# Loading the second head of every V tile through ScalarE's DMA queue in a decode attention kernel

## The chip, the core and the metric

The kernel runs on one core of a Trainium2 chip. A core has five engines that run side by side: TensorE (PE, matrix multiplication into PSUM), VectorE (DVE), ScalarE (ACT), GpSimd (POOL) and SyncE (SP). Data comes from device memory by DMA transfers, which SyncE or ScalarE issue, each into a queue of its own, and which 16 DMA engines carry out. The metric is the time of one execution in microseconds (us); lower is better.

## What is computed

One decode step of an attention block and of an MLP, both on the same normalised row, for a batch of four:

```
xn = layernorm(x)                          # x: 4 x 1 x 576
# attention: 32 query heads, 16 K/V heads, head size 128, the last 2048 positions of the cache
q = (xn @ wq) as 32 heads
p = softmax(q . k / sqrt(128))             # k: 4 x 16 x 2048 x 128, every K/V head serves 2 query heads
A = (p . v) @ wo                           # v as k
# MLP; with one position the shifted parts are zero, so x1 = xn
B = xn + gelu(layernorm(xn) @ w3) @ w4     # w3: 576 x 4608, w4: 4608 x 576
out = x + A + B
```

K and V of the window are 33.5 MB each in bf16; with the weights the kernel reads some 87 MB.

## The kernel before

All large loads go through a ring of four buffers of 4 MB, the pool `big`. In order they hold wq, K tile 0, half of w3, K tile 1, the rest of w3 with a part of w4, K tiles 2 to 7, V tiles 0 to 7, and the rest of w4 (`w4_end`). A load into a buffer can be issued only when the tile that was there four places earlier has been read: V tile 0 waits for the transposes of K tile 4, V tile 4 for the last matmul on V tile 0, and `w4_end` for V tile 4. A second, small pool holds the tiles of wo.

The work has three stages:

1. **K stage** (L518 to L535). For each of the eight K tiles of 4 MB, VectorE transposes it in four instructions (L298), and TensorE multiplies it with the queries (L305) into four banks of scores. Between them stand the products with w3, the gelu and a first part of w4.
2. **Softmax** (L154 to L201). ScalarE takes exponentials (L322), VectorE and ScalarE scale them (L343, L341), TensorE transposes them (L347), and VectorE and ScalarE copy them to the tile `PZ` (L355, L352).
3. **V stage** (L551 to L578). A V tile holds two heads, 2 MB each, loaded by one DMA each (L119 in `v_load`). The heads 0 to 15 go in order, and TensorE's order is written by hand (`manual_schedule`). For each head, `v_compute` runs 16 matmuls (L385), then `head_out` sums four diagonal blocks on VectorE (L422, L424), and one head later TensorE transposes the sum (L434). After four heads, `select` sorts the rows (L445 on TensorE, L453 and L454 on VectorE), and `project` multiplies with a tile of wo (L396). Selection and projection of heads 8 to 11 are placed behind head 12's matmuls and ahead of head 13's. Ahead of head 14's stand eight matmuls that fold partial sums (L561); the sums are copied by ScalarE (L555, L556).

At the end come the transposed sum and selection of heads 12 to 15, then the matmuls of `w4_end` and the last tile of wo (L414), the cast (L591) and the store (L592).

Apart from the small load of x (L98), every DMA is issued by SyncE, in program order: K tiles (L110), V (L119), wo (L405) and w4 (L573, L495). The V tiles 0 to 3 stand ahead of the softmax in the program, and tile 4 and later ones are issued behind heads 1, 3, 5 and 7. Completion is counted on eight semaphores that the loads use in turn, so a load also waits for the eighth before it to have landed.

Of the kernel before, what the change touches and what calls it, by code (L numbers as in the profile page):

```python
# [20 lines left out]
def kernel(  # L21
# [19 lines left out]
    nc = tc.nc  # L41
# [9 lines left out]
    G = 32  # L51
# [19 lines left out]
    v_win = A_v_cache[:, :, Sk - W:Sk, :]  # L71
# [43 lines left out]
    def v_load(pair):  # L115
        t = big.tile([P, 2, NCH, Dh], BF16, tag="big", name=f"v{pair}")
        for i in range(2):
            h = 2 * pair + i
            nc.sync.dma_start(out=t[:, i, :, :].rearrange("p c d -> p (c d)"),  # L119
                              in_=v_win[:, h].rearrange("b (p c) d -> p b (c d)", p=G))  # L120
            V_tiles[h] = t[:, i, :, :]

    wq_src = A_wq[0:KJ * P, :].rearrange("(p j) n -> p j n", j=KJ)
# [415 lines left out]
    for pair in range(NV0):  # L539
        v_load(pair)  # L540
        if pair % 2:
            load_wo(pair // 2)
    PZ = softmax()

    with tc.manual_schedule(engines={mybir.EngineType.PE}):
# [5 lines left out]
        for v in range(Hkv):  # L551
            run_projects()
            if v == Hkv - 3:
                sums = ktp.tile([P, DH], F32, tag="kt", name="sums")
                nc.scalar.copy(out=sums[0:64, :], in_=ACC[0:64, 0:DH])  # L555
                nc.scalar.copy(out=sums[64:P, :], in_=ACC2[64:P, 0:DH])  # L556
            if v == Hkv - 2:
                for q in range(2):
                    for z in range(2):
                        g = 2 * q + z  # L560
                        nc.tensor.matmul(out=ACC3[32 * g:32 * g + G, 0:DQ], lhsT=perm[:, q, :],  # L561
                                         rhs=sums[:, z * DQ:(z + 1) * DQ], start=False, stop=False, skip_group_check=True)
            v_compute(v)
            if selects:
                tsum, select = selects.pop()
                tsum()
                select()
            head_out(v)

            if v == 9:  # L570
                w4_end = big.tile([P, 2 * NFH - NE0, D], BF16, tag="big", name="w4_end")
                n0 = NFH - NE0
                nc.sync.dma_start(out=w4_end[:, 0:2 * n0, :].rearrange("p (e i) n -> p e (i n)", e=2), in_=w4_both)  # L573
                end = [(w4_end[:, e * n0:(e + 1) * n0, :], e, (1 - e) * NE0, n0) for e in range(2)]
            if v in (5, 9):
                load_wo((v + 3) // 4)
            if v % 2 and v // 2 + NV0 < Hkv // 2:
                v_load(v // 2 + NV0)  # L578
# [44 lines left out]
```

## Time and profile before

| | |
|---|---|
| Time, median of the runs shown | 213.42 us (213.35 to 213.48) |
| Time of the profiled execution | 213.12 us |
| Its span in the profile | 211.3 us |
| TensorE busy | 97.6 us (46%) |
| VectorE busy | 129.1 us (61%) |
| ScalarE busy | 17.8 us (8%) |
| Bytes read, mean rate | 87.17 MB, 413 GB/s |
| V loads at L119 | 16, 2048 KB each, 24.5 us from issue to landing (median) |

The span is what the profiler saw of the execution; 1.8 us lie around it. Busy shares are averages over stages with different limits, so they don't say which engine sets the time. For that one reads the slices (busy share of each engine in 40 equal parts of the span), the chain of waits (from the last instruction back to what released it) and the timeline of one engine, where the idle time before an instruction stands in brackets with what ended it. All times in these views are microseconds from the span's start.

### The profile page before, as it was taken

What the parts mean: (1) busy time and instruction counts of PE and PEld (TensorE: products, weight loads), DVE (VectorE), ACT (ScalarE), POOL (GpSimd) and SP (SyncE); (2) the same over time, 40 slices, a digit from 0 to 9 for tenths busy, and PEclk for the clock granted to TensorE, in tenths of its full rate; (3) what the DMA queues carried; (4) which work ended last, traced back from release to release, by engine and by line L of the source; (5) the groups of instructions that cost most, each with busy time, mean ns of one, the idle gap of its engine ahead of it and who ended that gap; (6) DMA issues with size and microseconds to landing.
All of it is one profiled execution on the core that took longest, in us unless ns stands there. A gap on an engine that the chain in (4) does not pass through costs nothing.

```text
span 211.3 us, 2591 instructions
## 1 busy us (share of the span) xinstructions
PE 97.6 (46%) x1099; PEld 49.8 (24%) x1099; DVE 129.1 (61%) x226; ACT 17.8 (8%) x36; POOL 1.8 (1%) x8
## 2 busy tenths in 40 slices
PE   1433159429703333423333330677499543553563
PEld 0110137408201011101111100543234221221252
DVE  7902692095359898879696951997836452135240
ACT  0003200000000000000000008951000000010000
POOL 2100000000000000000000000000000000000000
PEclk9999999999965555555555555589956785557555
DMA  7999999999999999999999999999999999999991
GB/s 299 397 471 422 406 450 394 449 410 470 409 447 434 406 453 428 416 459 416 416 425 403 440 426 433 412 437 431 418 419 431 426 419 428 437 406 428 422 386 49
DMA packets 5638, 87.32 MB, mean 413 GB/s; under 512 B 632, under 2 KB 636, under 8 KB 1532
## 3 DMA queue, kind: packets, MB, share of 16 engines
q1 hardware_dynamic: 5620, 87.17, 97.1%
q8 instruction: 8, 0.13, 0.3%
q14 instruction: 2, 0.02, 0.0%
q10 hardware_dynamic: 8, 0.00, 0.0%
HBM read 87.17 MB, written 0.00 MB: 413 GB/s over the span
## 4 chain that ended last, share of the span: by engine, by line
DMA 56%; DVE 27%; PE 8%; issue 4%; ACT 3%; SPq 1%; DVEq 0%; ACTq 0%
DMA k<-in_A_k_cache_dram 32%; DVE kt L298 19%; DMA w_end<-in_B_w_dram 12%; DMA v<-in_A_v_cache_dram 12%; PE S L305 4%; DVE prs L343 4%; PE O L385 2%; ACT E L322 2%; DVE osum L424 1%; DVE PZ L355 1%; DVE osum L422 1%; PE OT L434 1%; PE ACC L396 1%; PE pt L347 1%; SPq L136 1%
## 5 line engine op out<-in xcount | busy, mean ns | idle before, releaser
L298 DVE STREAM_TRANSPOSE kt<-k 128x2048 int32<-128x2048 int32 x32 | 71.1, 2279 | 15.9 <-DMA k<-in_A_k_cache_dram 15.9
L305 PE MATMUL S<-kt,qz 128*32 128x512 bf16 x256 | 30.4, 622 | 58.9 <-DVE kt L298 58.9
L385 PE MATMUL O<-v,PZ 128*32 128x512 bf16 x256 | 25.0, 513 | 12.9 <-DMA v<-in_A_v_cache_dram 12.1
L305 PEld LDWEIGHTS <-qz 128*32 128x32 bf16 x256 | 9.4, 127 | 75.8 <-issue 69.4
L422 DVE TENSOR_SCALAR osum<-O,diag 128x128 f32<-128x128 f32 x16 | 5.6, 349 | 22.7 <-PE O L385 22.7
L424 DVE SCALAR_TENSOR_TENSOR osum<-O,diag,osum 128x128 f32<-128x128 f32 x48 | 16.4, 345 | 0.8
L385 PEld LDWEIGHTS <-PZ 128*32 128x32 bf16 x256 | 7.2, 117 | 21.6 <-DMA v<-in_A_v_cache_dram 11.6
L322 ACT ACTIVATE E<-S,nb 128x256 f32<-128x256 f32 x8 | 4.5, 704 | 72.4 <-DVE nb L319 72.4
L347 PE MATMUL pt<-ident,prs 128*128 128x128 bf16 x64 | 5.9, 269 | 9.3 <-DVE prs L343 9.3
L434 PEld LDWEIGHTS OT<-sel,osum 128*128 128x128 f32 x32 | 6.2, 243 | 13.2 <-DVE osum L424 8.1
L434 PE MATMUL OT<-sel,osum 128*128 128x8 f32 x32 | 7.7, 314 | 3.2 <-DVE osum L424 3.2
L343 DVE TENSOR_SCALAR prs<-E,rdm 128x512 bf16<-128x512 f32 x12 | 8.0, 823 | 0.0
L347 PEld LDWEIGHTS <-prs 128*128 128x128 bf16 x64 | 5.2, 123 | 10.9 <-ACT prs L341 9.4
L317 DVE TENSOR_REDUCE mx<-S 128x1 f32<-128x512 f32 x4 | 2.8, 691 | 8.0 <-PE S L305 8.0
L478 PEld LDWEIGHTS <-w3a 128*128 128x128 bf16 x108 | 6.9, 166 | 1.7 <-issue 1.7
L478 PE MATMUL ACC<-ln2T,w3a 128*128 128x4 bf16 x108 | 7.0, 202 | 0.0
L396 PE MATMUL ACC<-wo,onx 128*4 128x288 bf16 x48 | 3.4, 433 | 7.4 <-DVE onx L454 7.4
L253 DVE CAST q_rows<-qp 128x256 bf16<-128x256 f32 x4 | 1.5, 418 | 8.5 <-PE qp L238 6.5
L436 DVE CAST on<-OT 128x8 bf16<-128x8 f32 x16 | 2.7, 166 | 5.6 <-PE OT L434 5.6
L238 PE MATMUL qp<-wq,xnT 128*8 128x512 bf16 x32 | 3.6, 628 | 3.6 <-DMA wq<-in_A_wq_dram 3.6
L341 ACT ACTIVATE prs<-E,rdm 128x512 bf16<-128x512 f32 x4 | 4.9, 1413 | 0.8 <-DVE rdm L329 0.8
L478 PEld LDWEIGHTS <-w3b 128*128 128x128 bf16 x72 | 4.5, 166 | 0.8 <-issue 0.8
(90 smaller groups left out, 67.3 us busy)
## 6 DMA issues: line engine op xcount, KB each, us to landing
k<-in_A_k_cache_dram SPq DMA_DIRECT2D x8, 4096.0 KB, 29.9
v<-in_A_v_cache_dram SPq DMA_DIRECT2D x16, 2048.0 KB, 24.5
wo<-in_A_wo_dram SPq DMA_DIRECT2D x4, 1152.0 KB, 29.8
wq<-in_A_wq_dram SPq DMA_DIRECT2D x1, 4096.0 KB, 12.7
w3a<-in_B_w_dram SPq DMA_DIRECT2D x1, 2304.0 KB, 26.8
w3b<-in_B_w_dram SPq DMA_DIRECT2D x1, 2304.0 KB
w_end<-in_B_w_dram SPq DMA_DIRECT2D x1, 2016.0 KB, 31.8
w3b<-in_B_w_dram SPq DMA_DIRECT2D x1, 1584.0 KB
```

What stands on the lines that cost most here:

```text
L298: nc.vector.transpose(out=ap32(kt[e], c0 * 2 * G, [[2 * G, C2 // 2], [1, 2], [2, G]]), in_=ap32(kn, c0 * 4 * G + e * G, [[4 * G, C2 // 2], ...
L305: nc.tensor.matmul(out=S[kq][c:c + 32, :].rearrange("p (c q l) -> p c q l", q=4, l=2), lhsT=qz[:, bp, m, y, :], rhs=kt[e][:, :, 4 * m:4 * ...
L322: nc.scalar.activation(out=E[:, :, g, x:GK:2].rearrange("p (c l) q -> p c q l", l=2), in_=S[g][:, 256 * x:256 * (x + 1)].rearrange("p (c q ...
L341: nc.scalar.mul(out=dst, in_=src, mul=rdm[:, b:b + 1])
L343: nc.vector.tensor_scalar_mul(out=dst, in0=src, scalar1=rdm[:, b:b + 1])
L347: nc.tensor.transpose(out=tp[:, cc, :], in_=pr[:, half * HC + cc, :, :, :].rearrange("p g k b -> p (g k b)"), identity=ident[:])
L385: nc.tensor.matmul(out=bank[G * j:G * j + G, :], lhsT=PZ[:, hp, c0:c0 + NI, :].rearrange("p c m -> p (c m)"), rhs=vn[:, c0:c0 + NI, :].rea ...
L396: nc.tensor.matmul(out=ACCS[half][o0:o0 + B, 0:DH], lhsT=lhsT, rhs=rhs_cols(q * DH, (q + 1) * DH), start=False, stop=False, skip_group_che ...
L422: nc.vector.tensor_scalar_mul(out=osum[:], in0=bank[:, 0:Dh], scalar1=diag[:, 0:1])
L424: nc.vector.scalar_tensor_tensor(out=osum[:], in0=bank[:, i * Dh:(i + 1) * Dh], scalar=diag[:, i:i + 1], in1=osum[:], op0=ALU.mult, op1=AL ...
L434: nc.tensor.matmul(out=OT[:, NB * o:NB * o + NB], lhsT=osum[:], rhs=sel[:], start=True, stop=True, skip_group_check=True)
L478: nc.tensor.matmul(out=gp[:, fc, :], lhsT=lhsT, rhs=rhs, start=False, stop=False, skip_group_check=True)
```

## The change

In `v_load`, the load of the second head of each V tile is issued by ScalarE instead of SyncE. The buffers, the bytes and the computation stay as they are.

```diff
         t = big.tile([P, 2, NCH, Dh], BF16, tag="big", name=f"v{pair}")
         for i in range(2):
             h = 2 * pair + i
-            nc.sync.dma_start(out=t[:, i, :, :].rearrange("p c d -> p (c d)"),
-                              in_=v_win[:, h].rearrange("b (p c) d -> p b (c d)", p=G))
+            queue = nc.scalar if i else nc.sync
+            queue.dma_start(out=t[:, i, :, :].rearrange("p c d -> p (c d)"),
+                            in_=v_win[:, h].rearrange("b (p c) d -> p b (c d)", p=G))
             V_tiles[h] = t[:, i, :, :]
```

In the built program ScalarE's eight new loads stand as follows: those of V tiles 0, 1 and 2 ahead of the exponentials (L322), that of tile 3 between the exponentials and the scaling (L341), and those of tiles 4 to 7 behind the last copy to `PZ` (L352) and ahead of the copies of L555 and L556. On SyncE the other loads keep their order. The semaphores still go round in program order over both queues. On VectorE all twelve scalings (L343) now stand ahead of the copies to `PZ` (L355), where before seven, three, one and one of them stood between these.

## The prediction

> **What bounds the kernel now.** I read the page's slices first, then the queues, the chain of waits, and TensorE's timeline at the end.
>
> ```profile
> DMA  7999999999999999999999999999999999999991
> ...
> q1 hardware_dynamic: 5620, 87.17, 97.1%
> ...
> q10 hardware_dynamic: 8, 0.00, 0.0%
> ```
>
> The 16 DMA engines are busy in every slice but the first and last, and one queue, SyncE's q1, carries all the data. ScalarE's queue q10 carried eight small packets, the load of x. So the time is 87 MB at some 428 GB/s, plus what follows the last landing. The chain of waits (start, us, what) says where it ends:
>
> ```profile
> 156.53 25.03 DMA v<-in_A_v_cache_dram
> 181.57 0.02 issue
> 181.58 26.28 DMA w_end<-in_B_w_dram
> 207.86 0.04 issue
> 207.91 0.46 PE ACC L414 x6
> 208.36 0.02 issue
> 208.38 0.31 DVE fin L591
> ```
>
> The last piece of w4 lands at 207.86, and only six small matmuls, the cast and the store follow. For every earlier transfer the computation finishes inside the time of the transfers behind it. Whether that stays true is the question, so the timeline of TensorE at the end counts (start, length, line, operation; in brackets the idle time before and what ended it):
>
> ```profile
> 181.61 1.90 PE L385 MATMUL O<-v,PZ 128*32 128x512 bf16 x16 [5.27 <-DMA v<-in_A_v_cache_dram]
> ...
> 187.15 1.13 PE L396 MATMUL ACC<-wo,onx 128*4 128x288 bf16 x16 [2.48 <-DVE onx L454]
> 188.07 1.92 PE L385 MATMUL O<-v,PZ 128*32 128x512 bf16 x16
> 189.92 0.39 PE L434 MATMUL OT<-sel,osum 128*128 128x8 f32 x2
> 190.24 0.45 PE L561 MATMUL ACC<-sums,perm 128*32 128x144 f32 x8
> 191.41 1.05 PE L385 MATMUL O<-v,PZ 128*32 128x512 bf16 x16 [0.72 <-DMA v<-in_A_v_cache_dram]
> ...
> 196.32 1.90 PE L385 MATMUL O<-v,PZ 128*32 128x512 bf16 x16 [3.55 <-DMA v<-in_A_v_cache_dram]
> ...
> 204.02 1.15 PE L414 MATMUL ACC<-wo,onx_q 128*32 128x144 bf16 x32 [0.92 <-DMA wo<-in_A_wo_dram]
> ```
>
> The four rows of L385 are heads 12 to 15. Each of 12, 14 and 15 starts the moment its half tile lands: v6's first half at 181.6, v7's halves at 191.4 and 196.3, one 2 MB half each 4.90 us. Between heads 12 and 13 stands the selection and projection of heads 8 to 11 (L454, L396): this makes 6.46 us of that step.
>
> **What the change does, part by part.**
>
> The listing of the changed program shows eight V loads moved from SyncE's order to ScalarE's. No byte, matmul or buffer is added, so the transfers together still take what they took: as long as no engine runs dry, the last byte still lands near 207.9. What changes is the *order* of landings.
>
> *Issue.* SyncE is rid of eight issues of 0.53 to 0.97 us (its rows at L119), all long ahead of their landing (14 to 34 us): nothing. ScalarE gains eight. Three stand before the exponentials (L322) and wait for the transposes of K tiles 4, 5 and 6 (numbered from 0); the exponentials wait for tile 7 anyway. The fourth stands between the exponentials and the scaling (L341), where ScalarE has 0.75 us idle: nothing. The other four stand after its last softmax copy (143.3) and wait for heads 1, 3, 5 and 7; behind them wait only the two copies of L555 and L556, needed at 188. Nothing.
>
> *Two rings.* Do transfers of a second queue wait behind the backlog of the first? The nearest case in the trace are instruction fetches, on q8, amid the loads. One of 16 KB, starting at 111.67, took 1.09 us, against 0.614 us for an undisturbed 16 KB packet of q1, while q1 had over 10 us of backlog. So a second ring is served at once and shares the engine about evenly, and the transfers ahead get about half speed. In the Trainium skill, "DMA: Bandwidth & Descriptors", section "Queues, rings and completion order", each DMA engine goes round robin between the rings that have work; these rows agree. Its section "Issuing engines are not separate DMA queues" says that issuing from several engines only saves issue time; read as a rule on time it speaks against any change here, and the sum by it would be 213.1.
>
> *Landings, stepped through with even sharing.* Rows: K tile 9.73 us, V half 4.90, wo 2.80 (differences of landings in the trace's records). From 89.2 each second half shares with K tiles that were queued ahead of it: K6 lands at 106.7 instead of 99.6, K7 at 121.0 instead of 109.4. VectorE transposes K at a fixed pitch:
>
> ```profile
> 91.81 8.88 DVE L298 STREAM_TRANSPOSE kt<-k 128x2048 int32<-128x2048 int32 x4
> ...
> 103.30 8.88 DVE L298 STREAM_TRANSPOSE kt<-k 128x2048 int32<-128x2048 int32 x4
> ...
> 114.79 8.88 DVE L298 STREAM_TRANSPOSE kt<-k 128x2048 int32<-128x2048 int32 x4
> ```
>
> so K6 starts at 106.8, not 103.3, and K7 at 121.1, not 114.8: the softmax comes 6.3 us late. That is hidden, because the transfers don't stop: everything issued before v4 keeps them busy until about 154, v4 is now issued at 144.66 + 6.3 = 150.9, and issue to first byte took 1.3 us in the store at the end. The cover is 154 - 150.9 - 1.3 = 1.8 us. VectorE's order inside the softmax also changes (all twelve scalings ahead of the copies to PZ); the same instructions, which I bound at ±1 us from the 0.5 us copies and the 0.6 us pitch of scalings: within the cover. The backlog of heads 0 to 11 then ends near 180, before it matters.
>
> *The tail, where it isn't hidden.* ScalarE's ring holds nothing but second halves, SyncE's also wo and the first halves. So the second halves run ahead: v6's and v7's second halves are served *before* v6's and v7's first halves end. v7's first half is still directly ahead of the 11.6 us of w4 and wo, so it lands at 196.3. v6's first half is directly ahead of it: 196.3 - 4.9 = 191.4, or up to 0.7 us earlier when v7's second half still shares with v7's first. I take **191.05 instead of 181.57** (low 190.7, high 191.4; other splittings that I stepped through, by packet or by whole transfer, give 191.3). Head 12 needs it, and the heads go in order, so nothing of heads 12 to 15 starts earlier, although the second halves lie there.
>
> From head 12's start the row gives 190.24 + 0.45 - 181.61 = 9.1 us until head 14 may start, now with no wait for data. Then head 14 to head 15: 1.4 us at the clock of the row at 191.41, 2.35 at the slower one (heads 6, 7 and 8 started at 156.94, 159.29 and 161.65). From head 15 to the last selection 203.65 - 196.32 = 7.3 us (VectorE's last L454 starts at 203.30 and takes 0.35), or 6.5 with 0.85 less for sixteen matmuls at the faster clock. Then the projection, 1.15, and 44 more matmuls at 1.87 / 56 us each, 1.5; all their weights have landed. Sum: 9.1 + 1.4 + 6.5 + 2.65 = 19.65 to 9.1 + 2.35 + 7.3 + 2.65 = 21.4; I take 20.6, between, since the granted clock switches between 0.5 and 1.0 in these stretches and nothing tells which comes.
>
> The last matmul then ends at 191.05 + 20.6 = 211.65 instead of 208.35: **+3.3 us** (low 190.7 + 19.65 - 208.35 = +2.0, high 191.4 + 21.4 - 208.35 = +4.45). Cast, store and end stay. The profiled run took 213.12 us (span 211.3 and 1.8 around it; the median of the runs shown is 213.42, 0.3 more): 213.12 + 3.3 = 216.4.
>
> *Rate of two rings.* Not shown by this trace. A 16 KB packet takes 0.614 us and a 32 KB one 1.216, so a packet has some 12 ns beside its bytes. If the second ring hid that for the 128 V packets of each engine, everything would land 1.5 us earlier; if switching cost as much again, 1.5 us later. I take 0 and keep both ends: 216.4 - 1.5 and + 1.5, and with the tail's bounds a range from 214.7 to 218.3.
>
> **Rivals.**
>
> *Order kept (not slower): 213.1.* If the rings are served in order of issue, or the share of the second is small, v6's first half still lands early. The point from which it decides is its landing at 208.35 - 20.6 = 187.7: earlier than that, the chain from head 12 ends under the last w4 transfer as now, and the price is nothing, or 1.5 us won if the packet gap is hidden (211.6). For it: all other counts are unchanged. Against it: the fetches that weren't held up. 0.10. The rule of the Trainium skill on issuing engines, quoted above by its section, comes out here too if it is read as a rule on time.
>
> *The transfers run dry: 218.5.* In the K stage the second halves delay the K tiles, the softmax and so v4's issue. If the softmax slips by over 6.3 + 1.8 = 8.1 us, the engines stand still before v4 comes, and each microsecond comes on top. With a slip of 10 us: 216.4 + 1.9, and somewhat more by the restart. For it: the cover is thin. Against: even the splitting that serves the second ring wholly first slipped no more than 6.3 in my steps. 0.08.
>
> *The change does nothing, since ScalarE issues late.* Excluded by its order: no issue stands behind work that ends later than the buffer comes free.
>
> **How the numbers follow.** Forecast 0.80, order kept 0.10, dry 0.08, the rest 0.02 (a rate beyond my bounds). The range 214.7 to 218.3 holds the forecast's bounds and the near part of the dry case; left out are order kept and the far part. Faster by over 0.2% (0.43 us, about what a measurement can tell) needs the order kept and a gap hidden: 0.04. Within it: 0.06. Slower: 0.90.
>
> **What would show it.** Right: q10 with 16.8 MB; the idle time before the exponentials longer by some 6 us; TensorE waits for V until about 191 and then runs heads 12 to 15 without a wait for data; the last w4 piece lands near 207.9 as now, but the matmuls of L414 end near 211.6, with VectorE's selection as the last releaser instead of a w_end transfer. Wrong: head 12 starts before 187.7; w_end still ends the chain; or a slice near 150 to 155 with DMA below 9.

## The result and the profile after

The changed kernel takes 216.62 us (median of 4 runs, 216.35 to 217.20) against 213.38 us (213.29 to 213.48): 3.2 us longer, a ratio of 1.0155 (95% interval 1.0143 to 1.0168). The forecast was 216.4, range 214.7 to 218.3. The profiled execution took 217.20 us with a span of 215.4, 4.1 us above that of before; it is the longest of the four, and times inside it are compared below with the profile of before.

The slices and queues of the changed kernel's page:

```profile
DMA  7999999999999999999998999999999999999930
...
q1 hardware_dynamic: 4468, 70.39, 76.9%
q10 hardware_dynamic: 1160, 16.78, 18.4%
```

16.78 MB now come through ScalarE's queue q10, as the change says. But for one slice with an eight, the DMA engines are as busy as before up to the last two slices of 5.4 us each; those hold three tenths and nothing, where before only the last slice was nearly empty: the transfers are over and the kernel isn't. (The change adds a line to the code, so the lines behind it are numbered one higher: L386 is the L385 of before.) The end of the chain of waits (start, us, what) shows what comes after them:

```profile
159.86 31.91 DMA v<-in_A_v_cache_dram
191.77 0.04 issue
191.81 1.90 PE O L386 x15
...
209.54 0.36 DVE onx_q L455
209.91 0.04 issue
209.95 2.50 PE ACC L415 x47
212.47 0.31 DVE fin L592
```

Before, the chain went over from a V load straight to the last piece of w4, and six matmuls ended it. Now it leaves the transfers at 191.77, when the first half of V tile 6 has landed, and for 20.7 us it is TensorE and VectorE alone. TensorE's timeline has the same stretch (in brackets the idle time before an instruction and what ended it):

```profile
191.81 1.90 PE L386 MATMUL O<-v,PZ 128*32 128x512 bf16 x16 [11.31 <-DMA v<-in_A_v_cache_dram]
...
197.35 1.13 PE L397 MATMUL ACC<-wo,onx 128*4 128x288 bf16 x16 [2.48 <-DVE onx L455]
198.26 1.92 PE L386 MATMUL O<-v,PZ 128*32 128x512 bf16 x16
...
201.12 1.81 PE L386 MATMUL O<-v,PZ 128*32 128x512 bf16 x16
...
203.18 1.05 PE L386 MATMUL O<-v,PZ 128*32 128x512 bf16 x16
...
209.95 1.15 PE L415 MATMUL ACC<-wo,onx_q 128*32 128x144 bf16 x32 [0.74 <-DVE onx_q L455]
210.88 1.53 PE L415 MATMUL ACC<-w_end,gTq 128*32 128x144 bf16 x44
```

Head 12 starts 10.2 us later than before (191.81 against 181.61) after an idle time of 11.31 us. Heads 13, 14 and 15 have no bracket with a DMA any more: by the landing records their data came at 181.96, 196.68 and 191.76, before their turn. The matmuls of L415 at the end, which waited for transfers three times before, run behind the selection and wait for none. By the trace's landing records the last piece of w4 came at 208.25, against 207.86.

### The profile page after: what moved, and what is told of

Same layout as the page of the kernel before. It is cut to its first block, busy times and chain, and to the rows that moved or that the text cites. A ratio compares the mean times of both kernels' runs of the same rounds, so it can differ in the third digit from the quotient of the medians.

```text
span 215.4 us, 2605 instructions
## 1 busy us (share of the span) xinstructions
PE 97.9 (45%) x1099; PEld 51.7 (24%) x1099; DVE 128.6 (60%) x226; ACT 17.7 (8%) x36; POOL 1.8 (1%) x8
## 3 DMA queue, kind: packets, MB, share of 16 engines
q10 hardware_dynamic: 1160, 16.78, 18.4%
## 4 chain that ended last, share of the span: by engine, by line
DMA 53%; DVE 20%; PE 20%; ACT 3%; issue 2%; ACTq 0%; SPq 0%; DVEq 0%
DMA k<-in_A_k_cache_dram 32%; DMA v<-in_A_v_cache_dram 15%; DVE kt L299 9%; DMA wq<-in_A_wq_dram 6%; PE O L386 6%; DVE prs L344 3%; PE ACC L479 3%; PE S L306 3%; ACT E L323 2%; PE qp L239 2%; DVE osum L425 2%; PE pt L348 2%; PE OT L435 1%; DVE tmp L454 1%; PE ACC L415 1%
## 5 line engine op out<-in xcount | busy, mean ns | idle before, releaser
L386 PE MATMUL O<-v,PZ 128*32 128x512 bf16 x256 | 25.0, 535 | 12.4 <-DMA v<-in_A_v_cache_dram 12.4
L386 PEld LDWEIGHTS <-PZ 128*32 128x32 bf16 x256 | 7.7, 122 | 20.6 <-DMA v<-in_A_v_cache_dram 12.2
L348 PE MATMUL pt<-ident,prs 128*128 128x128 bf16 x64 | 7.2, 309 | 10.5 <-DVE prs L344 8.5
L348 PEld LDWEIGHTS <-prs 128*128 128x128 bf16 x64 | 6.7, 143 | 11.6 <-ACT prs L342 9.4
L344 DVE TENSOR_SCALAR prs<-E,rdm 128x512 bf16<-128x512 f32 x12 | 7.1, 785 | 0.0
L397 PE MATMUL ACC<-wo,onx 128*4 128x288 bf16 x48 | 2.9, 385 | 7.2 <-DVE onx L455 7.2
```

The source lines that it names most:

```text
L344: nc.vector.tensor_scalar_mul(out=dst, in0=src, scalar1=rdm[:, b:b + 1])
L348: nc.tensor.transpose(out=tp[:, cc, :], in_=pr[:, half * HC + cc, :, :, :].rearrange("p g k b -> p (g k b)"), identity=ident[:])
L386: nc.tensor.matmul(out=bank[G * j:G * j + G, :], lhsT=PZ[:, hp, c0:c0 + NI, :].rearrange("p c m -> p (c m)"), rhs=vn[:, c0:c0 + NI, :].rea ...
```

## The experiments

The theory: the second halves of V tiles 6 and 7, in a ring (the list of waiting transfers of one queue) of their own, are served ahead of the first half of V tile 6 or in turn with it; head 12 waits for it, and the heads go in order, so the chain from head 12 to the end outlasts the w4 transfers. Its rivals: (A) the K tiles and the softmax come late; (B) two rings move fewer bytes in the same time; (C) the loss goes with the number of transfers that pass. All six kernels compute the whole result. The kernel before was run beside them, with medians of 213.23 us (beside the first four kernels) and 213.25 us. Ratios are to these, with their 95% interval.

### The halves change places

```diff
-            queue = nc.scalar if i else nc.sync
+            queue = nc.sync if i else nc.scalar
```

> The halves change places: the first head of every V tile comes through ScalarE's queue, the second through SyncE's. Main theory (the loss is the chain behind the landing of v6's first half): first halves now run ahead, so head 12 starts near 182 and the selection of heads 8 to 11 is over before 189; v6's second half lands near 191.5 and v7's near 196.5, heads 13 to 15 need no selection between them, and TensorE ends within 0.5 us of the last w4 landing: 213.3 to 214.0. Rival A (the delay of the K stage and of the softmax costs the time): the same eight transfers run beside the K tiles, so 216.6 again. Rival B (two rings move fewer bytes in the same time): 216.6 again, with the last w4 landing near 211.

Measured: 213.21 us, ratio 0.9996 (0.9986 to 1.0005). As many bytes go through ScalarE's queue, the first halves in place of the second, and the loss is gone. TensorE's timeline of this kernel:

```profile
180.95 1.90 PE L386 MATMUL O<-v,PZ 128*32 128x512 bf16 x16 [0.41 <-DMA v<-in_A_v_cache_dram]
...
187.04 1.13 PE L397 MATMUL ACC<-wo,onx 128*4 128x288 bf16 x16 [2.24 <-DVE onx L455]
191.73 1.90 PE L386 MATMUL O<-v,PZ 128*32 128x512 bf16 x16 [3.56 <-DMA v<-in_A_v_cache_dram]
...
208.21 0.43 PE L415 MATMUL ACC<-w_end,gTq 128*32 128x144 bf16 x8 [0.15 <-DMA w_end<-in_B_w_dram]
```

A half of V tile 6 is late here too (191.7), but it is head 13's. The selection behind head 12 has been done in the meantime, and the last row again waits for w_end. Rivals A and B, which foresaw 216.6, fall: the last K tile landed at 117.36, as late as in the changed kernel (117.13; 109.37 in the kernel before), and the last piece of w4 at 208.16.

### Only V tiles 0 to 3 through ScalarE's queue

```diff
-            queue = nc.scalar if i else nc.sync
+            queue = nc.scalar if i and pair < 4 else nc.sync
```

> Only the second halves of V tiles 0 to 3 go through ScalarE's queue. Main theory: the last two V tiles land as in the kernel before (v6's first half near 181.6), so 213.3 to 213.8, although K tile 7 lands late and v4 is issued some 4 us late. Rival A (K stage and softmax): nearly the whole loss, 216 to 216.6. Rival B (rate of two rings): half of it, about 215.

Measured: 213.32 us, ratio 1.0005 (0.9996 to 1.0014). VectorE's timeline of this kernel shows that the K stage does come late, as in the changed kernel:

```profile
103.21 8.88 DVE L299 STREAM_TRANSPOSE kt<-k 128x2048 int32<-128x2048 int32 x4
...
117.32 8.89 DVE L299 STREAM_TRANSPOSE kt<-k 128x2048 int32<-128x2048 int32 x4 [2.54 <-DMA k<-in_A_k_cache_dram]
```

The last K tile is transposed from 117.3 on, 2.5 us later than before, and nothing of it reaches the end: head 12 starts at 181.75. This is the delay of rival A alone, at no cost. V tile 4 was issued at 146.61, only 2.0 us later than in the kernel before and not some 4 as expected.

### Only V tiles 6 and 7 through ScalarE's queue

```diff
-            queue = nc.scalar if i else nc.sync
+            queue = nc.scalar if i and pair >= 6 else nc.sync
```

> Only the second halves of V tiles 6 and 7 go through ScalarE's queue. Main theory: both pass v6's first half, which lands at 191 or a little later, so 216.0 to 217.0. Rival A (K stage and softmax, which are untouched here): 213.4. Rival B (rate of two rings, a quarter of the bytes): about 214.2.

Measured: 216.16 us, ratio 1.0163 (1.0137 to 1.0189): 2.9 us, nearly the loss of the whole change, from two of its eight transfers. The K stage is that of the kernel before (last K tile at 109.28). In the landing records, v6's second half landed at 171.53 and v7's at 181.35, both ahead of v6's first half at 191.49. TensorE's timeline shows the chain behind that landing, and no transfer that ends a wait in it:

```profile
191.54 1.90 PE L386 MATMUL O<-v,PZ 128*32 128x512 bf16 x16 [5.27 <-DMA v<-in_A_v_cache_dram]
...
208.89 1.15 PE L415 MATMUL ACC<-wo,onx_q 128*32 128x144 bf16 x32 [1.54 <-DVE onx_q L455]
209.82 1.54 PE L415 MATMUL ACC<-w_end,gTq 128*32 128x144 bf16 x44
```

### Only V tile 7 through ScalarE's queue

```diff
-            queue = nc.scalar if i else nc.sync
+            queue = nc.scalar if i and pair == 7 else nc.sync
```

> Only the second half of V tile 7 goes through ScalarE's queue. Main theory: one half of 4.9 us passes v6's first half, which lands at 186.5, before the point of 187.7 from which the chain of heads 12 to 15 outlasts the w4 loads; so 213.3 to 213.9. Rival C (the loss is in proportion to the transfers that pass it): half the loss, about 215. Rival A: 213.4.

Measured: 213.28 us, ratio 1.0002 (0.9993 to 1.0011). One transfer passes instead of two, v6's first half lands 5 us late instead of 10, and the loss is not half but nothing. So rival C falls: there is a point up to which the delay is free. TensorE's timeline shows this kernel close to it:

```profile
186.80 1.90 PE L386 MATMUL O<-v,PZ 128*32 128x512 bf16 x16 [5.27 <-DMA v<-in_A_v_cache_dram]
...
206.34 1.15 PE L415 MATMUL ACC<-wo,onx_q 128*32 128x144 bf16 x32 [0.74 <-DVE onx_q L455]
207.27 1.22 PE L415 MATMUL ACC<-w_end,gTq 128*32 128x144 bf16 x44
```

The chain from head 12 ends at 208.49, where before the w4 landing at 207.86 put the end at 208.35. Both ways of ending are level here, and it is already the chain that ends last: the matmuls with wo wait for the selection, not for a transfer. In the kernel with V tiles 6 and 7 head 12 starts 4.7 us later still, and the time is 2.9 us longer; the rest is the chain itself, which took 21.7 us here and 19.8 there. The sixteen matmuls of head 14 took 1.90 us here and 1.03 there, those of head 15 1.90 and 1.05: the granted clock (the share of TensorE's full speed that it was given) was 0.50 here from 196 to 201 us and 1.00 there from 200.6 to 207.

### The selection of heads 8 to 11 ahead of head 12

To the changed kernel, with all its transfers, this is added:

```diff
+            if v == 12:
+                tsum, select = selects.pop()
+                tsum()
+                select()
+                run_projects()
             v_compute(v)
             if selects:
```

> All second halves go through ScalarE's queue, as in the change; in addition the selection and projection of heads 8 to 11 stand ahead of head 12's matmuls instead of behind them, where TensorE idles for 11 us. No transfer is touched. Main theory (the loss is the length of the chain behind v6's first half): the chain from head 12 on loses the 4 us of selection and projection, heads 12 to 15 follow each other at 2.35 us, and TensorE ends at 191.8 + 7.5 + 7.3 + 2.65 = 209.2 or, at the faster clock, just behind the last w4 piece: 213.3 to 214.2, although v6's first half still lands near 191.7. Rivals A and B (K stage, rate of two rings), which see no change in the transfers: 216.6.

Measured: 213.26 us, ratio 1.0000 (0.9991 to 1.0009). In TensorE's timeline the selection and projection have moved into the idle time:

```profile
184.12 0.37 PE L446 MATMUL OT<-on,pick 128*32 128x32 bf16 x8 [0.26 <-DVE on L437]
186.60 1.13 PE L397 MATMUL ACC<-wo,onx 128*4 128x288 bf16 x16 [2.11 <-DVE onx L455]
191.61 3.61 PE L386 MATMUL O<-v,PZ 128*32 128x512 bf16 x32 [3.88 <-DMA v<-in_A_v_cache_dram]
```

V tile 6's first half is as late as in the changed kernel (191.57), yet heads 12 and 13 now follow each other in one row of 32 matmuls, 3.61 us in place of the 8.37 from 191.81 to 198.26 + 1.92. TensorE ends at 206.81 + 1.72 = 208.53, close to the 208.35 of the kernel before. The late landing alone costs nothing: what cost time is the work that was lined up behind it.

### The same earlier place in the kernel before

The same five lines in the kernel before, with every load on SyncE.

> The kernel before, with the same earlier place of that selection and no load moved. Main theory: the end is set by the last w4 landing, so nothing is gained: 213.1 to 213.5. If the selection had been on the path before as well, it would come out lower by up to 2 us, 211.5.

Measured: 213.25 us, ratio 1.0001 (0.9992 to 1.0010). The last row of TensorE that waits is the one for w4, as before:

```profile
207.95 0.43 PE L414 MATMUL ACC<-w_end,gTq 128*32 128x144 bf16 x8 [0.16 <-DMA w_end<-in_B_w_dram]
```

Where the last landing sets the end, a shorter chain gains nothing. So the gain in the kernel above is the removal of this change's loss, and no version tried is faster than the kernel before.

## Why the prediction was right

**Bytes and end of the transfers: right.** The prediction had them end near 207.9 as before. They ended at 208.25 in the changed kernel, and between 207.97 and 208.16 in the experiments with a second ring. The term for the rate of two rings, taken as 0 with 1.5 us on either side, came to at most 0.4 us by the last landing. In the Trainium skill, "DMA: Bandwidth & Descriptors", section "Issuing engines are not separate DMA queues", queues share the same engines and a second one only saves issue time; on the bytes moved, the trace agrees with this. As a rule on the time it doesn't hold here, because the order of landings changed.

**Order of landings: right, 0.7 us short.** Head 12's data was put at 191.05 (bounds 190.7 to 191.4) and landed at 191.77, outside the bounds. It landed one whole half, 4.9 us, ahead of v7's first half, so the "up to 0.7 us earlier", of which the prediction took half, did not come; and v7's first half landed at 196.68 instead of 196.28, 0.4 us late like the pieces of w4 behind it. The 16 DMA engines lay further apart: the first of them was done with the last piece of w4 at 205.87, as before (205.91), the last 0.4 us later than before. For head 12's data the first was done at 188.74, 3.0 us ahead of the last, where in the kernel before it was 2.0 us. The prediction had carried the spread of before over; what widened it is not shown.

**The chain from head 12: right.** 20.6 us were forecast, between 19.65 and 21.4. In the profile TensorE's last matmul ends at 210.88 + 1.53 = 212.41, 20.60 after 191.81. The terms in us: to head 14, 9.1 forecast and 9.31 measured; from 14 to 15, 1.4 to 2.35 and 2.06; from 15 to the last selection, 6.5 to 7.3 and 6.72; the matmuls behind it 2.65 and 2.50.

**The number: in part luck.** In the profiles the time grew by 4.1 us where 3.3 was forecast: head 12 started 0.76 us later than forecast, and the chain took its 20.6. The other three executions were 0.5 to 0.9 us shorter than the profiled one and have no trace, so why the median came within 0.2 us of the forecast is not shown. The range of 214.7 to 218.3 is also narrower than the two bounds added up, which give 213.6 to 219.1.

**The point of decision: right as far as it was bracketed.** It was worked out as a landing of head 12's data at 187.7. At 186.75 nothing was lost, at 191.49 2.9 us were. The point itself was not measured, and it moves with the chain: with V tile 7 alone the chain took 21.7 us, 0.3 above the forecast's upper bound (0.28 of it a wait for v7's first half), and ended 0.14 us behind that of the kernel before although the landing was 0.95 us ahead of 187.7.

**The K stage: right that it is hidden, wrong in size.** The step that failed is "shares the engine about evenly". It gave a softmax 6.3 us late; the changed kernel's VectorE shows

```profile
103.10 8.88 DVE L299 STREAM_TRANSPOSE kt<-k 128x2048 int32<-128x2048 int32 x4
...
117.23 8.89 DVE L299 STREAM_TRANSPOSE kt<-k 128x2048 int32<-128x2048 int32 x4 [2.56 <-DMA k<-in_A_k_cache_dram]
```

a start of K tile 7 at 117.23, 2.4 us later than before, and no delay of tile 6. So the sign "idle time before the exponentials longer by some 6 us" did not come: 75.03 us against 72.36.

Two things were missed. In the packet records, packets of both rings kept their undisturbed lengths, 1.216 us for 32 KB of K and 0.614 us for 16 KB of V, and joined end to end (the records don't name the engine) one of K and one of V follow each other: the rings take turns by packet, not by bytes, so between 94 and 100 us K got 1.61 MB and V 1.00 MB. The Trainium skill says so too, in "Queues, rings and completion order" of the same page (turns at packet granularity), though a packet there is typically 9 to 17 descriptors, and that one packet of the profile is so many isn't shown here. The prediction had read the longer instruction fetch as sharing by bytes. And the second ring's first packet began at 93.57, 4.5 us after the issue at 89.04, not at once. What held it up isn't settled by these runs: three or four 32 KB packets already accepted from the first ring would fill that time, but with V tile 7 alone, where 16 KB packets stood there, it was 4.1 us too (issue 159.81, first packet 163.94), nearly seven of those.

The failed step cost the forecast nothing, because v6's first half was counted back from the last landing, and at the end the V packets of both rings are 16 KB long, so that turns by packet and by bytes come out alike.

V tile 4 was issued at 148.78, 4.1 us late instead of 6.3. The first exponential came 2.5 us late. The rest is not the order of VectorE's scalings, which the prediction had bounded at 1 us (from copies of 0.5 us; in the kernel before they took 0.69 to 0.81): with V tiles 0 to 3 alone that order is the same and K tile 7 as late, and V tile 4 was issued only 2.0 us late. From 142 to 149 us the granted clock was 0.57 in the changed kernel and 1.00 in that one; the second 32 transposes of the softmax took 3.57 us against 1.95, and the 32 matmuls behind them 3.08 against 2.45, which makes the difference between the two. The transfers did not run dry, as forecast: the slices at 150 to 155 hold nines, and the cover, counted as in the prediction, was 154 - 148.78 - 1.3 = 3.9 us instead of 1.8.

**The rivals.** "Order kept" did not happen, but its point of decision stands between the kernel with V tile 7 alone and that with V tiles 6 and 7. "Dry" did not happen either.

## What to carry to other kernels

When the DMA engines are busy throughout, as here, moving loads to a second queue changes little in what they move, but it changes the order of landings: a load in a short queue takes turns with what waits in a long one, and doesn't wait behind it. Look for the consumer that is first in program order and last in landing, and measure the work lined up behind it against the transfers that are still to come; up to the point where the two end together the delay is free, and beyond it it shows. The cure is to give the faster queue what is needed first, or to move work that does not need the late data ahead of the wait.

## What the runs showed of the hardware

Two rings with work alternate by packet (0.614 us for 16 KB, 1.216 us for 32 KB, neither lengthened), so the ring with the larger packets gets the larger share (1.61 MB against 1.00 in 6 us). A second ring that is filled while the first has a backlog got its first packet 4.5 us after the issue (4.1 in the kernel with V tile 7 alone), far ahead of that backlog of two K tiles, 9.7 us each. In the changed kernel the landings of one transfer on the 16 engines lay 3.0 to 3.7 us apart for the first halves of V tiles 4 to 6 (1.7 to 1.8 for those of tiles 1 to 3), against 1.9 to 2.0 in the kernel before. What waits for the transfer waits for the last of them. Why they spread is not shown.
